# One 129-column product with v per key group, summed in two rounds per head, in an attention and channel-mix kernel on one core

## The chip, the core and the metric

The kernel runs on one core of a Trainium2 chip. Its time is device microseconds of one execution of the whole program, and each version is judged by the median of its runs. The profile is one more execution, recorded by the hardware profiler; times inside it are microseconds from the start of its span.

## The reference: what is computed

For 8 batches of 8 heads, queries are averaged in pairs (1152 to 576), attention runs against 1152 keys of 64 columns, and the result, 576 rows of 512 columns per batch, goes through a gated channel mix.

```python
q_pool = q.reshape(B, H, S // factor, factor, D).mean(axis=3)
scores = scale * np.matmul(q_pool, k.transpose(0, 1, 3, 2))
scores = scores - np.max(scores, axis=-1, keepdims=True)
attn = np.exp(scores)
attn = attn / (np.sum(attn, axis=-1, keepdims=True) + 1e-09)
attn_out = np.matmul(attn, v)
...
xk = mu_k * x + (1.0 - mu_k) * x_prev
xr = mu_r * x + (1.0 - mu_r) * x_prev
k = np.maximum(xk @ w_k, 0.0)
v = k * k @ w_v
r = 1.0 / (1.0 + np.exp(-(xr @ w_r)))
return (r * v).astype(np.float32)
```

## The kernel before

All inputs are float32; the matmuls take float16 operands, so each float32 factor is split into a high and a low half and a product is a sum of two or three matmuls.

**Order.** Every step is recorded with `op` (engine, an estimated duration, what it reads and writes, a due time `key`). At the end `Issue.run` plays the recorded steps against the estimated durations and hand-over times in `LAT`, in several rounds, keeps the order with the least planned total and issues every engine's instructions in that order. `LATE` and `SLACK` lengthen the estimates, `SEED` and `SPREAD` disturb the due times of the first round. Each engine then takes its instructions strictly in the planned order, so an instruction that waits holds back all behind it on its engine.

**Scores.** `block` handles 96 queries of one head against all 1152 keys (9 groups of 128); a head has 6 blocks, the program 384. TensorE forms the scores (L462, 9 matmuls of 96 columns) in one of three PSUM tiles `s`. VectorE takes the maximum over the key groups (L469), TensorE turns it (L472), VectorE reduces it to one value per query (L475), TensorE spreads its negative (L477), ScalarE writes it as a row of the low half of the queries (L480), TensorE adds the low products and the shift (L486), and ScalarE takes the exponential into `pf` (L492). `pf` holds 32-bit words whose upper 16 bits are read as the high float16 weight; GpSimd makes the low weight `pl` from the lower 16 bits (L494).

**Product with v.** `window` handles 128 queries; a head has 5 windows (`WIN`). Per key group, the high weights are loaded twice: once for a matmul of 65 columns (L513: the high half of v and a column of ones, whose sum is the denominator) and once for one of 64 columns (L515: the low half of v), both added into the same 65 columns of the PSUM bank `a`. The low weights multiply `vb`, a scaled float16 copy of v with its ones column, in 65 columns (L520). All five windows of a head lie side by side in the bank (5 x 65 = 325 columns). After the fifth, VectorE adds a guard to the denominators (L535), inverts them (L537) and writes the quotients to `xb` (L538). After every second head, TensorE turns the pair (L550) and ScalarE copies it to `xt` (L553). In the first batch (heads 0 to 7) the odd heads use the bank `f` instead (`ALT`).

**Preparation.** `prep` loads k and v of a head. ScalarE makes the high half `kn` (L415) and VectorE the rest (L418), in two pieces of 5 and 4 groups; for the first 8 heads GpSimd makes the rest (`KN_POOL`). `vt` holds v as [low 64 | high 64 | ones] (L428, L431), `vb` is made by GpSimd (L434).

**Weights.** `weights` loads the three weight matrices in 20 pieces of 512 64-bit numbers a row and rebuilds float32 from the two words: ScalarE L580 into `ex` and L587 into `em`, VectorE joins them (L590) and adds the sign (L598), ScalarE rounds to the high half (L600) and GpSimd makes the low half (L601). `ex` and `em` are in SBUF, two buffers each.

**Channel mix.** `ff` works on tiles of 256 rows as soon as a batch's attention is complete, so nothing of it can run during the first batch. Its matmuls of 256 and 512 columns (L665) go to the bank `f`, and after the last batch to all banks in turn. They are what TensorE has to do between the steps of the blocks.

## Time and profile before

| | |
|---|---|
| median of 3 runs | 1162.75 us (1162.2 to 1163.17) |
| the profiled execution, its own time | 1164.27 us |
| its span | 1162.5 us |
| granted TensorE clock, mean | 0.997 |
| TensorE matmuls | 19504, busy 1111.6 us (96%) |
| TensorE weight loads | 19504, busy 926.0 us (80%) |
| VectorE | 908.2 us busy (78%) |
| ScalarE | 888.7 us busy (76%) |
| GpSimd | 550.0 us busy (47%) |

In the profile PE is TensorE, PEld its weight loads, DVE VectorE, ACT ScalarE, POOL GpSimd and SP the engine that issues the transfers; L with a number is a line of the kernel. Matmuls are pipelined: the duration shown for one is from its start to its modelled end, and what a matmul takes of the engine is the distance between its start and the next one's. A row of the timeline is start, duration, engine, line, operation and operands, number merged. A row of the groups is line, engine, operation, operands with shapes, count, then busy time and mean duration in ns, then the engine's idle time just before and what ended it. A row of the windows is the stretch, its length, then each engine's busy time with its number of instructions, then the clock.

### The profile page before, as it was taken

The numbers are of one execution on the slowest core, as the hardware profiler recorded it, in microseconds if no ns is written. First come the engines' busy times: TensorE is split into PE (matmuls) and PEld (weight loads), VectorE is DVE, ScalarE is ACT, GpSimd is POOL, SyncE is SP. The second block draws the span as 40 slices with busy tenths as digits, with TensorE's granted clock in tenths as the row PEclk, the third lists the DMA queues.
The fourth block names the chain that finished last, engine by engine and source line by source line (L and its number), as shares of the span: only waits on it lengthen the run. The fifth ranks groups of instructions, "written<-read, shape, count | busy, mean of one in ns | idle before, by whom it ended". The sixth has DMA issues, their size and how long they took to land.

```text
span 1162.5 us, 45688 instructions
## 1 busy us (share of the span) xinstructions
PE 1111.6 (96%) x19504; PEld 926.0 (80%) x19504; DVE 908.2 (78%) x1791; ACT 888.7 (76%) x1838; POOL 550.0 (47%) x565
## 2 busy tenths in 40 slices
PE   4887799999999999999999999999999999999998
PEld 3776687978788887988788888979797978888565
DVE  6898878888888878888888878787888788774530
ACT  4988797887878788778877787878778778765743
POOL 4787554544445453544444453535354545443111
PEclk9999999999999999999999999999999999999999
DMA  9956663565545363564355536455554445310000
GB/s 233 219 143 175 155 135 78 134 130 126 129 99 114 94 143 98 134 123 106 90 109 120 132 81 145 85 117 115 113 123 86 95 112 93 70 30 10 20 19 28
DMA packets 222380, 126.69 MB, mean 109 GB/s; under 512 B 157664, under 2 KB 194528, under 8 KB 222176
## 3 DMA queue, kind: packets, MB, share of 16 engines
q1 hardware_dynamic: 222176, 123.77, 47.1%
q8 instruction: 152, 2.49, 0.9%
q14 instruction: 52, 0.43, 0.1%
HBM read 67.11 MB, written 9.44 MB: 66 GB/s over the span
## 4 chain that ended last, share of the span: by engine, by line
PE 85%; ACT 6%; DVE 3%; DMA 2%; issue 2%; POOL 1%; SPq 0%; DVEq 0%; ACTq 0%
PE f L665 33%; PE s L462 11%; PE s L486 11%; PE a L520 6%; PE a L515 6%; PE a L513 6%; PE s L665 4%; ACT pf L492 2%; PE s L472 2%; PE a L665 2%; DVE mx L469 1%; PE s L477 1%; PE a L550 1%; DMA st<-in_moe_w_k_dram 1%; ACT qT L480 1%
## 5 line engine op out<-in xcount | busy, mean ns | idle before, releaser
L494 POOL TENSOR_SCALAR pl<-pf 128x864 f16<-128x864 uint16 x384 | 385.0, 1003 | 405.4 <-ACT pf L492 378.3
L469 DVE TENSOR_REDUCE mx<-s 128x96 f16<-128x864 f32 x384 | 401.5, 1054 | 102.7 <-PE s L462 59.9
L492 ACT ACTIVATE pf<-s 128x864 int32<-128x864 f32 x384 | 337.4, 890 | 70.5 <-PE s L486 45.8
L462 PE MATMUL s<-qT,ks 128*128 128x96 f16 x3456 | 221.2, 207 | 28.6 <-DMA qT<-qn 15.1
L462 PEld LDWEIGHTS <-ks 128*128 128x128 f16 x3456 | 185.5, 99 | 54.6 <-issue 22.9
L515 PE MATMUL a<-vt,pf 128*128 128x64 f16 x2700 | 227.6, 194 | 0.0
L513 PE MATMUL a<-vt,pf 128*128 128x65 f16 x2700 | 227.2, 193 | 0.0
L486 PE MATMUL s<-qT,ks 128*128 128x96 f16 x3456 | 214.5, 207 | 7.2 <-ACT qT L480 6.7
L513 PEld LDWEIGHTS <-pf 128*128 128x128 f16 x2880 | 204.1, 99 | 6.0 <-ACT pf L492 0.4
L486 PEld LDWEIGHTS <-ks 128*128 128x128 f16 x3456 | 180.9, 98 | 28.5 <-issue 7.7
L515 PEld LDWEIGHTS <-pf 128*128 128x128 f16 x2880 | 194.8, 98 | 7.8 <-issue 0.3
L480 ACT ACTIVATE qT<-s 1x96 f16<-1x96 f32 x384 | 91.9, 243 | 99.8 <-PE s L477 87.6
L475 DVE TENSOR_REDUCE mb<-s 96x1 f16<-96x128 f32 x384 | 108.6, 285 | 57.9 <-PE s L472 53.3
L520 PE MATMUL a<-vb,pl 128*128 128x65 f16 x2700 | 143.4, 193 | 0.5 <-POOL pl L494 0.5
L665 PE MATMUL f<-xhk,wk_hi 128*128 128x256 f16 x496 | 135.1, 272 | 1.3 <-ACT xt L553 0.8
L665 PE MATMUL f<-xhk,wk_lo 128*128 128x256 f16 x496 | 135.1, 272 | 0.0
L665 PE MATMUL f<-xlk,wk_hi 128*128 128x256 f16 x496 | 135.1, 272 | 0.0
L520 PEld LDWEIGHTS <-pl 128*128 128x128 f16 x2880 | 121.8, 98 | 7.9 <-POOL pl L494 1.2
L696 POOL TENSOR_TENSOR gl<-g 128x512 f16<-128x512 f32 x72 | 78.5, 1090 | 100.7 <-ACT g L694 98.3
L665 PEld LDWEIGHTS <-wk_hi 128*128 128x128 f16 x1152 | 106.2, 98 | 11.6 <-issue 1.5
L472 PE MATMUL s<-identb,mx 128*96 128x128 f16 x384 | 87.1, 227 | 4.9 <-DVE mx L469 4.5
L665 PE MATMUL f<-wv_hi,g 128*128 128x512 f16 x240 | 90.9, 379 | 0.3 <-ACT ex L713 0.2
(101 smaller groups left out, 1990.2 us busy)
## 6 DMA issues: line engine op xcount, KB each, us to landing
kr<-in_k_dram SPq DMA_DIRECT2D x64, 288.0 KB, 3.3
vr<-in_v_dram SPq DMA_DIRECT2D x64, 288.0 KB, 3.1
qr<-in_q_dram SPq DMA_DIRECT2D x32, 320.0 KB, 3.7
ks<-ks SPq DMA_DIRECT2D x64, 144.0 KB, 2.8
out_dram<-em SPq DMA_DIRECT2D x36, 256.0 KB, 2.4
qr<-in_q_dram SPq DMA_DIRECT2D x32, 256.0 KB, 3.4
st<-in_moe_w_k_dram SPq DMA_DIRECT2D x8, 512.0 KB, 4.9
st<-in_moe_w_v_dram SPq DMA_DIRECT2D x8, 512.0 KB, 4.1
```

The costliest lines, as they stand in the source:

```text
L462: nc.tensor.matmul(cols(c, c + 1), ks1[hp][:, c, :], qhi, start=(c == c0), stop=False, skip_group_check=True)
L469: op("DVE", 0.967, lambda: nc.vector.tensor_reduce(mxz, grid(0, NC).rearrange("p c q -> p q c"), axis=AX.X, op=ALU.max), r=[("s", z)], w=[ ...
L472: op("PE", 0.057, lambda: nc.tensor.matmul(s[0:QN, 0:P], mxz, identb, start=False, stop=False, skip_group_check=True), r=[("mx", z)], w=[( ...
L475: op("DVE", 0.199, lambda: nc.vector.tensor_reduce(mbz[0:QN], s[0:QN, 0:P], axis=AX.X, op=ALU.max), r=[("s", z)], w=[("mb", z)], key=t + O ...
L480: op("ACT", 0.133, lambda: nc.scalar.activation(qlo[QN:QN + 1], s[QN:QN + 1, 0:QN], AF.Prelu, scale=1.0 - EPS, alpha=(1.0 + EPS) / (1.0 - ...
L486: nc.tensor.matmul(cols(c, c + 1), ks2[hp][:, c, :], qlo, start=False, stop=True, skip_group_check=True)
L492: op("ACT", NC * QN / 1200 + 0.051, lambda: nc.scalar.activation(pf[:, :, rows], grid(0, NC), AF.Exp, bias=SHIFT, scale=0.125 / (2.0 * SQ) ...
L494: op("POOL", NC * QN / 1000 + 0.12, lambda: nc.gpsimd.tensor_scalar(pl[:, :, rows], half(pf, U16, 0)[:, :, rows], LO, 1.0, op0=ALU.mult, o ...
L513: nc.tensor.matmul(bank[:, a0:a0 + VN], half(pf, F16, 1)[:, c, rows], vt[jv][:, c, D:D + VN], start=(w == 0 and c == 0), stop=False, skip_ ...
L515: nc.tensor.matmul(bank[:, a0:a0 + D], half(pf, F16, 1)[:, c, rows], vt[jv][:, c, 0:D], start=False, stop=False, skip_group_check=True)
L520: nc.tensor.matmul(bank[:, a0:a0 + VN], pl[:, c, rows], vb[jv][:, c, 0:VN], start=False, stop=(c == NC - 1), skip_group_check=True)
L665: nc.tensor.matmul(ps, terms[i][0], terms[i][1], start=(first and i == 0), stop=(i == last), skip_group_check=True)
```

## The change

It does five things at once.

1. From head 8 on (`SPLIT`), the two high matmuls per key group become one of 129 columns: v's low half, its high half and the ones are neighbours in `vt`. The low and the high half now stand in different columns, a window takes 129 columns, and a bank holds three windows. So a head is summed in two rounds, windows 0 to 2 and 3 to 4. After each, ScalarE copies the low columns to SBUF (`xlb`, L562), VectorE adds them to the high ones in PSUM (L564) and then divides (L566), with guard (L557) and inversion (L559) per round. The next round begins only when the bank has been read.
2. Heads 0 to 7 keep the two matmuls, but all of them use the bank `a` (`ALT` 0).
3. In those heads VectorE makes the rest of k (`KN_POOL` 0; 16 instructions move from GpSimd) and ScalarE makes `vb` (`VB_ACT`; 8 instructions move from GpSimd).
4. The weights are rebuilt through the bank `f`, which is idle in the first batch: the first ScalarE step writes there, VectorE joins there (L623) and adds the sign from there into `ex` (L626). There is one such bank, where `ex` and `em` have two buffers.
5. The planner's estimates, margins, seed and spread are others, so the whole order is new.

```diff
-LATE, SLACK = 0.08, 0.1
-KN_POOL, VT_POOL, XL_POOL = 8, 0, 0
-DEC_K, DEC_RV = "D", "D"
-ALT = 1
+LATE, SLACK = 0.04, 0.05
+KN_POOL, VT_POOL, XL_POOL = 0, 0, 0
+DEC_K, DEC_RV = 'S', 'S'
+ALT = 0
+VB_ACT = 8
+SPLIT = 8
...
-SEED, SPREAD = 2, 1.0
+SEED, SPREAD = 0, 3.0
...
+        if n < VB_ACT:
+            op("ACT", NC * D / 1200 + 0.093, lambda: nc.scalar.activation(
+                vb[j][:, :, 0:D], vr[i], AF.Copy, scale=SV * VLO), r=[("vr", i)], w=[("vb", j)], key=key + 4)
...
+        two = int(n >= SPLIT)
+        k0, k1 = [x[:2] for x in TURN if x[0] <= w < x[1]][0] if two else (0, NW)
+        VW = VN + two * D
+        a0, rows = (w - k0) * VW, slice(r0, r0 + P)
...
+                if two:
+                    nc.tensor.matmul(bank[:, a0:a0 + VN + D], half(pf, F16, 1)[:, c, rows], vt[jv][:, c, 0:VN + D],
+                                     start=(w == k0 and c == 0), stop=False, skip_group_check=True)
+                    continue
...
-        if w < NW - 1:
+        if w < k1 - 1:
             return
...
+        if two:
+            xl_ = xl_b[0][:, 0:k1 - k0]
+            op("ACT", 0.051 + (k1 - k0) * D / 1200, lambda: nc.scalar.copy(xl_, u[:, :, 0:D]),
+               r=[ka], w=[("xlb",)], key=t + O_EVAC)
+            op("DVE", 0.07 + (k1 - k0) * D / 960, lambda: nc.vector.tensor_tensor(
+                u[:, :, D:2 * D], u[:, :, D:2 * D], xl_, op=ALU.add), r=[ka, ("xlb",)], w=[ka], key=t + O_EVAC)
...
+                    ep, kf = f_b.bitcast(I32), ("f",)
...
+                    op("ACT", 0.52, lambda wh=wh: nc.scalar.activation(f_b, wh.bitcast(F32), AF.Abs, scale=2.0 ** -111),
+                       r=[ks], w=[kf], key=key)
...
+                        v_(0.6, lambda mi=mi, ep=ep: nc.vector.scalar_tensor_tensor(
+                            ep, ep, 3, mi, op0=ALU.logical_shift_left, op1=ALU.bitwise_or), [kf, km], [kf], False)
+                        kd, ed = (ke, e) if dec == "S" else (kf, f_b)
+                        v_(0.6, lambda ep=ep, wh=wh, ed=ed: nc.vector.scalar_tensor_tensor(
+                            ed.bitcast(I32), wh, -0x80000000, ep, op0=ALU.bitwise_and, op1=ALU.bitwise_or), [ks, kf], [kd], False)
```

Three places of the planned order show what moves. On TensorE, two key groups of one window of the product with v, in a later head, stood so before (`pf` are the weights that are loaded, `vt` what is multiplied):

```order
L513 LDWEIGHTS pf
L513 MATMUL a<-vt_86,pf 128x65
L515 LDWEIGHTS pf
L515 MATMUL a<-vt_86,pf 128x64
L513 LDWEIGHTS pf
L513 MATMUL a<-vt_86,pf 128x65
L515 LDWEIGHTS pf
L515 MATMUL a<-vt_86,pf 128x64
```

On TensorE now, the end of one window's high products and the first of its low ones:

```order
L531 LDWEIGHTS pf
L531 MATMUL a<-vt_87,pf 128x129
L531 LDWEIGHTS pf
L531 MATMUL a<-vt_87,pf 128x129
L541 LDWEIGHTS pl
L541 MATMUL a<-vb_90,pl 128x65
```

Four weight loads and four matmuls have become two of each; the low products are as they were.

On VectorE, the evacuation of head 30 before (`mx` and `mb` are the maxima of a block, `xb` the quotients):

```order
L475 TENSOR_REDUCE mb_96<-s_132 96x1
L535 TENSOR_SCALAR den_99<-a 128x5
L537 RECIPROCAL den_99<-den_99 128x5
L538 TENSOR_TENSOR xb_101<-a,den_99 128x5x64
L469 TENSOR_REDUCE mx_94<-s_133 128x96
```

On VectorE now, the first round of the same head (the second follows ten rows later with 2 windows in place of 3):

```order
L477 TENSOR_REDUCE mx_93<-s_133 128x96
L557 TENSOR_SCALAR den_99<-a 128x3
L701 TENSOR_TENSOR xlk_109<-xm_106,xhk_111 128x256
L559 RECIPROCAL den_99<-den_99 128x3
L564 TENSOR_TENSOR a<-a,xlb_102 128x3x64
L483 TENSOR_REDUCE mb_96<-s_133 96x1
L566 TENSOR_TENSOR xb_101<-a,den_99 128x3x64
L477 TENSOR_REDUCE mx_95<-s_135 128x96
```

Three steps per head have become eight, and other work stands between them.

On VectorE in the first batch, around the 18th block, before (`ex`, `em` and `st` belong to the weights):

```order
L469 TENSOR_REDUCE mx_95<-s_134 128x96
L590 SCALAR_TENSOR_TENSOR ex_120<-ex_120,em_122 128x512
L475 TENSOR_REDUCE mb_98<-s_134 96x1
L469 TENSOR_REDUCE mx_93<-s_132 128x96
L598 SCALAR_TENSOR_TENSOR ex_120<-st_124,ex_120 128x512
L475 TENSOR_REDUCE mb_96<-s_132 96x1
L469 TENSOR_REDUCE mx_94<-s_133 128x96
```

On VectorE now, around the same block:

```order
L477 TENSOR_REDUCE mx_95<-s_135 128x96
L483 TENSOR_REDUCE mb_97<-s_134 96x1
L422 TENSOR_TENSOR kn_76<-kr_70,kn_76 128x4x64
L435 SCALAR_TENSOR_TENSOR vt_86<-vr_72,vt_86 128x5x64
L483 TENSOR_REDUCE mb_98<-s_135 96x1
L435 SCALAR_TENSOR_TENSOR vt_86<-vr_72,vt_86 128x4x64
L623 SCALAR_TENSOR_TENSOR f<-f,em_123 128x512
L422 TENSOR_TENSOR kn_77<-kr_71,kn_77 128x5x64
L626 SCALAR_TENSOR_TENSOR ex_121<-st_125,f 128x512
L477 TENSOR_REDUCE mx_93<-s_133 128x96
```

The rest of k (L422) has come from GpSimd, and the weights pass through `f`.

More of the change, by code (lines that the diff above doesn't have):

```diff
@@ L465, in block @@
         for c0, c1 in BK:
-            op("PE", (c1 - c0) * 0.0424, lambda c0=c0, c1=c1: scores(c0, c1),
+            op("PE", (c1 - c0) * 0.0430, lambda c0=c0, c1=c1: scores(c0, c1),
                r=[("ks1", hp)] + kh, w=[("s", z)], key=t)
-        op("DVE", 0.967, lambda: nc.vector.tensor_reduce(mxz, grid(0, NC).rearrange("p c q -> p q c"),
+        op("DVE", 0.975, lambda: nc.vector.tensor_reduce(mxz, grid(0, NC).rearrange("p c q -> p q c"),
                                                          axis=AX.X, op=ALU.max),
            r=[("s", z)], w=[("mx", z)], key=t)
-        op("PE", 0.057, lambda: nc.tensor.matmul(s[0:QN, 0:P], mxz, identb, start=False, stop=False,
+        op("PE", 0.059, lambda: nc.tensor.matmul(s[0:QN, 0:P], mxz, identb, start=False, stop=False,
                                                  skip_group_check=True),
@@ L519, in lo @@
             for c in range(c0, c1):
-                nc.tensor.matmul(bank[:, a0:a0 + VN], pl[:, c, rows], vb[jv][:, c, 0:VN],
+                nc.tensor.matmul(bank[:, a0 + two * D:a0 + two * D + VN], pl[:, c, rows], vb[jv][:, c, 0:VN],
                                  start=False, stop=(c == NC - 1), skip_group_check=True)
         for c0 in (0, 3, 6):
-            op("PE", 3 * 0.0582, lambda c0=c0: hi(c0, c0 + 3),
-               r=vk + [("pf", j) for j in js] + ([ka] if c0 or w else []), w=[ka], key=t)
+            op("PE", 3 * (0.0565 if two else 0.0606), lambda c0=c0: hi(c0, c0 + 3),
+               r=vk + [("pf", j) for j in js] + ([ka] if c0 or w > k0 else []), w=[ka], key=t)
@@ L543, in window @@
-        for k0, k1, q0 in TURN:
-            base = WIN[k0][0]
-            qe = WIN[k1 - 1][0] + P
-            def turned(k0=k0, k1=k1, base=base):
-                for k_ in range(k0, k1):
+        dz, xz, d0 = den[z][:, k0:k1], xb[0][:, k0:k1], two * D
+        xk = [("xb", hh, x[0]) for x in TURN if k0 <= x[0] < k1]
+        op("DVE", 0.075, lambda: nc.vector.tensor_scalar(dz, u[:, :, d0 + D], GUARD, None, op0=ALU.add),
+           r=[ka], w=[("den", z, k0)], key=t + O_EVAC)
+        op("DVE", 0.08, lambda: nc.vector.reciprocal(dz, dz), r=[("den", z, k0)], w=[("den", z, k0)], key=t + O_EVAC)
@@ new lines, in window @@
+        if two:
[4 more added lines that the diff above has]
+                u[:, :, D:2 * D], u[:, :, D:2 * D], xl_, op=ALU.add), r=[ka, ("xlb",)], w=[ka], key=t + O_EVAC)
+        op("DVE", 0.07 + (k1 - k0) * D / 960, lambda: nc.vector.tensor_tensor(
+            xz[:, :, hh], u[:, :, d0:d0 + D], dz.unsqueeze(2).broadcast_to([P, k1 - k0, D]), op=ALU.mult),
+           r=[("den", z, k0), ka], w=xk, key=t + O_EVAC)
@@ L549, in turned @@
+        if hh == 0 or w < NW - 1:
+            return
+        for t0, t1, q0 in TURN:
+            base = WIN[t0][0]
+            qe = WIN[t1 - 1][0] + P
+            def turned(t0=t0, t1=t1, base=base):
+                for k_ in range(t0, t1):
                     r_ = WIN[k_][0] - base
-                    nc.tensor.transpose(bank[:, r_:r_ + P], xz[:, k_].rearrange("p h d -> p (h d)"), ident)
-            op("PE", 0.11 * (k1 - k0), turned, r=[("xb", 0), ("xb", 1)], w=[ka], key=t + O_TURN)
+                    nc.tensor.transpose(bank[:, r_:r_ + P], xb[0][:, k_].rearrange("p h d -> p (h d)"), ident)
+            op("PE", 0.113 * (t1 - t0), turned, r=[("xb", 0, t0), ("xb", 1, t0)], w=[ka], key=t + O_TURN)
@@ L581, in weights @@
+                op("ACT", 0.565, lambda e=e, wh=wh: nc.scalar.activation(e, wh.bitcast(F32), AF.Abs, scale=2.0 ** -111),
                    r=[ks], w=[ke], key=key)
@@ L688, in ff @@
                               (wlo["k"][:, c, fs], hk[:, c, 0:n], r)]
[L689 removed]
+                products(pv[:, f - f0], pk, terms, n / 2400.0 + 0.0025, first=(f == f0))
             z = turn("r32")
```

69 lines of the change are left out of this document (44 added, 25 removed).

## Prediction

> **What bounds the kernel now.** I read the windows first, cut where the channel mix begins and where the attention ends. The columns after the length are TensorE, its weight loads, VectorE, ScalarE, GpSimd, then the granted clock.
>
> ```profile
> 0.00:145.00 145.00, 103.10 (x2142) 92.98 (x2143) 121.69 (x227) 113.60 (x224) 94.50 (x101) 0.98 0.77 185
> 145.00:1075.00 930.00, 924.92 (x16845) 782.15 (x16843) 757.01 (x1506) 730.37 (x1521) 442.72 (x453) 1.00 0.48 105
> 1075.00:1162.50 87.50, 83.60 (x522) 50.88 (x520) 29.47 (x58) 44.69 (x95) 12.83 (x12) 1.00 0.06 24
> ```
>
> There are three stages. From 145 to 1075 us TensorE is busy 924.92 of 930 us; VectorE has 81% there and ScalarE 79%. The end is channel mix alone, again TensorE. In the first 145 us TensorE has 71% and VectorE leads with 84%. So a nanosecond off TensorE counts in full only after 145 us, and before that only the others count.
>
> Next the waits of TensorE inside the first 145 us (waited for: us, times, longest):
>
> ```profile
> PE s L462 <- DMA qT<-qn: 15.1, 1, 15.1
> PE s L462 <- ACT pf L492: 11.1, 22, 1.4
> PE s L486 <- ACT qT L480: 6.5, 12, 2.6
> PE s L472 <- DVE mx L469: 3.9, 8, 0.8
> ```
>
> After 15.1 us of loading, TensorE waits for the loop of a block itself: a free tile `s`, the written shift, the maximum. With three tiles, a block there advances as fast as VectorE and ScalarE take it round, and the channel mix is not there yet to fill in.
>
> Then the timeline of TensorE in the saturated stage, for what a matmul costs start to start:
>
> ```profile
> 602.00 0.27 PE L665 MATMUL f<-xhk,wk_lo 128*128 128x256 f16 x1
> ...
> 602.66 0.22 PE L472 MATMUL s<-identb,mx 128*96 128x128 f16 x1
> ...
> 604.24 0.19 PE L513 MATMUL a<-vt,pf 128*128 128x65 f16 x1
> 604.27 0.19 PE L515 MATMUL a<-vt,pf 128*128 128x64 f16 x1
> ...
> 604.60 0.44 PE L520 MATMUL a<-vb,pl 128*128 128x65 f16 x9
> 604.87 0.33 PE L462 MATMUL s<-qT,ks 128*128 128x96 f16 x4
> 605.04 0.55 PE L486 MATMUL s<-qT,ks 128*128 128x96 f16 x9
> 605.42 0.19 PE L513 MATMUL a<-vt,pf 128*128 128x65 f16 x1
> 605.45 0.20 PE L515 MATMUL a<-vt,pf 128*128 128x64 f16 x1
> ...
> 605.98 0.23 PE L472 MATMUL s<-identb,mx 128*96 128x128 f16 x1
> ```
>
> Six matmuls of 256 columns take 602.00 to 602.66, 110 ns each; nine of 96 columns 605.04 to 605.42, 42.2 ns; nine of 65 columns 604.60 to 604.87, 30.0 ns. The six pairs from 604.24 to 604.60 take 60.0 ns each, the nine pairs from 605.42 to 605.98 take 62.2 ns. Each of these matmuls has its own weight load, which by itself lasts 99 ns and overlaps the matmuls and loads before it:
>
> ```profile
> L513 PEld LDWEIGHTS <-pf 128*128 128x128 f16 x2880 | 204.1, 99 | 6.0 <-ACT pf L492 0.4
> ```
>
> **Part 1, the pairs.** 56 heads x 5 windows x 9 groups = 2520 pairs become single matmuls of 129 columns. No row has this width behind its own kind; the line through 96 and 256 columns rises (110 - 42.2) / 160 = 0.424 ns a column and gives 42.2 + 33 x 0.424 = 56.2 ns at 129. Against 60.0 the saving is 3.8 ns a pair, 9.6 us in all; against 62.2 it is 6.0 ns, 15.1 us. I take 12 us: the 65-column row at 30.0 speaks for the lower end, nine pairs against six for the upper. All of it lies after 145 us, on the path: **-12.0 us** (-9.6 to -15.1).
>
> The Trainium skill (TensorE: Matmul & The Clock Gate, section Back-to-back issue gap) gives about 81 ns per matmul at 128 columns in a stream of weight load and matmul; by that this part would be an estimated +50 us, not -12. The 42.2 ns row at 96 columns, each with its load, does not agree with it.
>
> **Part 2, what two rounds add in the saturated stage.** These rows carry it:
>
> ```profile
> L538 DVE TENSOR_TENSOR xb<-a,den 128x320 f32<-128x320 f32 x60 | 29.2, 487 | 1.3
> L729 DVE SCALAR_TENSOR_TENSOR em<-f,ex 128x512 f32<-128x512 f32 x30 | 20.7, 688 | 4.0 <-PE f L665 3.2 <-PE s L477 0.4
> L537 DVE RECIPROCAL den<-den 128x5 f32<-128x5 f32 x64 | 11.9, 186 | 1.4
> L535 DVE TENSOR_SCALAR den<-a 128x5 f32<-128x5 f32 x60 | 9.5, 158 | 11.4 <-PE a L520 10.5 <-PE s L477 0.4
> L553 ACT COPY xt<-a 128x384 f32<-128x384 f32 x28 | 13.4, 480 | 8.2 <-PE a L550 7.8
> L553 ACT COPY xt<-a 128x192 f32<-128x192 f32 x28 | 9.0, 322 | 1.9 <-PE a L550 1.5
> L513 PE MATMUL a<-vt,pf 128*128 128x65 f16 x2700 | 227.2, 193 | 0.0
> ```
>
> An elementwise step that reads PSUM costs 487 ns at 320 columns and 688 at 512: 1.05 ns a column, so 353 ns at 192 and 286 at 128. Per head VectorE gets two additions (639 ns), division in two pieces (639 in place of 487) and a second guard and inversion (344): 1.14 us, times 56 is 64 us. ScalarE gets a copy of 192 columns (322 ns) and one of 128 (by its two rows 269): 0.59 us, times 56 is 33 us. The stage then has VectorE at 821 of 918 us (89%) and ScalarE at 83%: both under TensorE, so the work itself costs nothing while TensorE has other matmuls queued.
>
> The wait is the question. The first product of the second round is queued on TensorE in order, and if the bank isn't read by then, all scores and channel mix behind it wait. The path of a round is copy 322, addition 353, division 353 ns and three hand-overs, about 1.2 us when both engines are free; up to 1.9 us more if a maximum and an exponential (about 1 us each) stand ahead. The cover is what the new order puts between the last low product of window 2 and the first product of window 3: counted in matmuls at the pitches above, 1.9 us in the worst two heads, 2.6 to 3.2 in twenty, median 3.5, up to 7.4. Before, the same bank between heads cost nothing (idle 0.0 ahead of L513). So no stall in most heads, some tenths in a few: 0 to 6 us, I take **+1.5 us**, near the row of zero.
>
> **Part 3, the first stage.** What moves in there, by these rows:
>
> ```profile
> L590 DVE SCALAR_TENSOR_TENSOR ex<-ex,em 128x512 int32<-128x512 int32 x20 | 16.0, 802 | 1.1 <-ACT ex L580 1.1
> L598 DVE SCALAR_TENSOR_TENSOR ex<-st,ex 128x512 int32<-128x512 int32 x20 | 14.4, 720 | 0.0
> L418 DVE TENSOR_TENSOR kn<-kr,kn 128x320 f16<-128x320 f32 x56 | 31.1, 555 | 0.9 <-ACT kn L415 0.8
> L418 DVE TENSOR_TENSOR kn<-kr,kn 128x256 f16<-128x256 f32 x56 | 25.3, 452 | 0.0
> L418 POOL TENSOR_TENSOR kn<-kr,kn 128x320 f16<-128x320 f32 x8 | 8.6, 1080 | 3.6 <-ACT kn L415 3.4
> L418 POOL TENSOR_TENSOR kn<-kr,kn 128x256 f16<-128x256 f32 x8 | 5.4, 676 | 1.9 <-ACT kn L415 1.5
> L434 POOL TENSOR_SCALAR vb<-vr 128x576 f16<-128x576 f32 x64 | 43.8, 684 | 73.9 <-PE a L520 45.7 <-PE s L477 13.0 <-DMA vr<-in_v_dram 8.4
> L385 ACT ACTIVATE qn<-qs 128x640 f16<-128x640 f32 x32 | 23.4, 733 | 3.3 <-DMA qT<-qn 2.1 <-DVE qs L382 1.0
> L636 DVE SCALAR_TENSOR_TENSOR xm<-xt,mu_k,tmp 128x256 f32<-128x256 f32 x48 | 27.9, 590 | 1.0 <-ACT tmp L633 0.5
> ```
>
> GpSimd loses 8 x (1080 + 676 + 684) ns = 19.5 us; it is at 65% there and gates little. VectorE gains 16 pieces of k, 8 x (555 + 452) = +8.1 us. The weights read one of their two operands from PSUM now; the nearest row for that is L729 at 688, so a piece costs 1.38 in place of 1.52 us. Up to the 54th maximum the new order has 19 pieces where the old has 16: 19 x 1.38 - 16 x 1.52 = +1.8 us; and five fewer steps of the mix (at the 590 of L636 or less), -2.7. VectorE's sum: +7.2 on 121.7 us. ScalarE gains 8 `vb` (about 0.68 each, a little under L385's 640 columns): +5.4.
>
> The Trainium skill (SBUF — State Buffer, section Who interferes with whom) says that a VectorE instruction with two SBUF inputs is held up by a GpSimd instruction that reads SBUF. The 802 of L590 against the 688 of L729 agrees: the rebuilt weights escape it, the 16 pieces of k enter it.
>
> If VectorE kept its share of 84%, 7.2 us of work would be 8.6 us of time; if the gaps take it, 0. The long runs of channel mix also begin later: before, they begin at the 55th block,
>
> ```profile
> 149.16 0.54 PE L462 MATMUL s<-qT,ks 128*128 128x96 f16 x9 [0.64 <-ACT pf L492]
> ```
>
> and in the new order with the 60th. A block of the first stage takes (149.16 - 15.1) / 54 = 2.48 us, and TensorE idles 29% of that: five more such blocks cost up to 3.6 us. Against this stands what a better order of the stage can save; the worst stretch of before is
>
> ```profile
> 90.00:100.00 10.00, 7.86 (x182) 7.24 (x183) 8.75 (x16) 9.29 (x18) 7.62 (x7) 1.00 0.74 189
> 100.00:110.00 10.00, 6.18 (x116) 5.47 (x114) 9.51 (x20) 7.46 (x18) 6.31 (x7) 0.91 0.74 193
> ```
>
> where TensorE falls to 6.18 of 10 us with VectorE at 9.51; without it some 2 us would be back, and with the relieved GpSimd perhaps as much again. Bounds: -4 to +12. I take **+5 us**, under half of 8.6 + 3.6, since VectorE had 16% of gaps. One bank `a` for the first eight heads and one bank `f` for the weights are counted in this range: evacuating took 0.8 us (158 + 186 + 487 ns) a head.
>
> **The sum.** -12.0 + 1.5 + 5.0 = -5.5 us. The profiled execution took 1164.27 us (span 1162.5), so it would take 1158.8; it stands 1.5 us above the median of the runs, so the forecast is 1157.2, said as **1157**.
>
> **The rivals.** (a) The first stage is not longer, or shorter: VectorE's gaps take the extra work and the relieved GpSimd hands `pl` over sooner. For it: nothing waits long for VectorE there (3.9 us). Then 1164.3 - 12 + 1.5 - (0 to 4) - 1.5 = 1148 to 1152 us. (b) Slower: VectorE bounds the first eight heads. With its use unchanged, 7.2 us of work and the later fill give the whole 12.2, and from VectorE above 90% on, a few more for each maximum that stands behind a piece of k; then -12 + 1.5 + 14 = +3.5, 1166 us. It decides where the first stage loses more than 12 - 1.5 = 10.5 us, which is 3.6 of later fill and a block of 2.6 us in place of 2.48. For it: VectorE at 84% and 9.51 of 10 in the worst stretch; against it: GpSimd's and TensorE's waits are shorter. (c) The evacuation in mid-head stalls TensorE: if the path takes 3.3 us as a rule, 24 heads wait some 0.5 us each, 11.6 us in all in place of 1.5: -12 + 11.6 + 5 = +4.6, 1167 us. Against it: the order leaves 3.5 us at the median, and before, the steps of an evacuation add up to 0.8. (d) The weight load is no longer hidden behind the one longer matmul and sets its pitch, 99 ns: 2520 x (99 - 61) = +96 us and the rest as forecast, about 1265 us. Against it: today two loads and two matmuls go by in 61 ns.
>
> **How the numbers follow.** The forecast's case (1152 to 1161) has 0.55, (a) 0.20, (b) 0.16, (c) 0.07, (d) 0.02. About 0.2% (2.3 us) is what a measurement of this kernel can tell from no change. Faster: 0.49 of the forecast's 0.55 and all of (a), 0.69. Same: 0.06 of the forecast's, 0.04 of (b), 0.02 of (c), 0.12. Slower: the rest of (b), (c) and (d), 0.19. The range 1146 to 1166 reaches down to (a) with a larger saving per pair and up to (b); (d) and half of (c) and of (b) lie outside.
>
> **What would show it.** Right: the new L531 stands 56 ns apart and the stage after the first batch takes about 10 us less; TensorE's share there stays over 99%; idle ahead of L531 is at most 1.5 us; VectorE near 89% there. The 60th block begins by 166 us, at most 5 us after the place that the old pace gives it, 15.1 + 59 x 2.48 = 161 us. Wrong: a pitch over 60 ns; waits of L531 for VectorE of 5 us or more; a first stage over 12 us longer or shorter than said.

## The result, and the profile after

| | before | after |
|---|---|---|
| median of the runs shown with the result | 1162.47 us (1162.0 to 1163.17, 4 runs) | 1174.91 us (1173.58 to 1177.36, 4 runs) |
| ratio | | 1.0108 (95%: 1.0095 to 1.0120) |
| profiled execution | 1164.27, span 1162.5 | 1174.88, span 1173.1 |
| granted clock, mean | 0.997 | 0.989 |
| TensorE matmuls | 19504 | 16984 |

The change makes the kernel 12.4 us slower; 1157 us was forecast, with 1166 as the end of the range. The engine totals of the page after read:

```profile
PE 1116.5 (95%) x16984; PEld 920.7 (78%) x16984; DVE 943.8 (80%) x2087; ACT 913.5 (78%) x1958; POOL 522.8 (45%) x541
```

VectorE is busy 35.6 us longer, ScalarE 24.8, GpSimd 27.2 less. The same three windows as before (stretch, length, busy time of TensorE, its loads, VectorE, ScalarE and GpSimd, clock, DMA share, GB/s):

```profile
0.00:145.00 145.00, 103.29 (x2117) 93.85 (x2118) 121.59 (x241) 118.54 (x233) 70.31 (x78) 0.93 0.77 192
145.00:1075.00 930.00, 919.29 (x14236) 768.64 (x14236) 789.71 (x1776) 745.22 (x1622) 437.34 (x450) 1.00 0.47 104
1075.00:1173.10 98.10, 93.97 (x634) 58.20 (x631) 32.47 (x70) 49.78 (x106) 15.18 (x15) 0.99 0.06 22
```

In the saturated stage TensorE is idle 10.7 of 930 us, where it was 5.1. VectorE stands at 85% there, ScalarE at 80%: neither is full. The wider matmul itself does what was asked of it; the timeline of TensorE in a late head shows nine of them in a row:

```profile
709.52 0.44 PE L541 MATMUL a<-vb,pl 128*128 128x65 f16 x9
709.80 0.67 PE L531 MATMUL a<-vt,pf 128*128 128x129 f16 x9
710.31 0.44 PE L541 MATMUL a<-vb,pl 128*128 128x65 f16 x9
710.58 0.23 PE L480 MATMUL s<-identb,mx 128*96 128x128 f16 x1
```

From 709.80 to 710.31 is 56.7 ns each; over the whole trace the mean is 56.6. The Trainium skill (TensorE: Matmul & The Clock Gate, section Back-to-back issue gap) also gives, for the gap of a matmul by itself, a rule of columns divided by 2.4 GHz plus 2.5 ns, an estimated 56.3 ns here. The trace agrees with it at 56.6, although each of these matmuls has its own weight load.

What TensorE waits for between 170 and 1062 us (engine, line, waited for: us, times, longest; the loads are the first to feel a wait). Before:

```profile
PEld L462 <- issue: 2.4, 7, 0.5
PEld L472 <- DVE mx L469: 2.2, 6, 0.6
PEld L486 <- issue: 1.8, 6, 0.4
PEld L477 <- DVE mb L475: 1.0, 2, 0.7
...
PE s L472 <- DVE mx L469: 0.7, 2, 0.4
PE s L477 <- DVE mb L475: 0.6, 1, 0.6
```

After:

```profile
PEld L470 <- issue: 7.6, 23, 0.7
PEld L494 <- issue: 5.5, 21, 0.7
PEld L480 <- DVE mx L477: 5.3, 17, 0.7
PEld L485 <- DVE mb L483: 4.1, 14, 0.7
PEld L531 <- issue: 2.2, 6, 0.8
...
PEld L531 <- DVE xb L566: 0.7, 3, 0.4
```

The loads of the same four steps of a block (both score products, the turning of the maxima and the spreading of the negative) wait 22.5 us where they waited 7.4. Of the 22.5, 13.1 stand as issue, for which the profile names no cause, and 9.4 are waits for the two maxima. The loads of the new matmul L531, where the forecast looked for a stall, wait 2.9. The waits of the four steps are short, 0.3 us at the mean and 0.7 at most, and spread over the stage.

**An account of the whole span.** From the starts of all matmuls I worked out how much each step from one matmul to the next is longer than the measured pitches, the distances from start to start, allow (0.417 ns a column + 2.5 ns, which gives the 42.5, 109.2 and 215.8 ns measured at 96, 256 and 512 columns; twice that for a float32 transpose). "Need" is the sum of these pitches, "idle" the rest (time lost to a lower clock is in it), cut at the 61st block, the first of the second batch (170.2 us before, 176.7 after); 108 channel-mix matmuls had been issued by then in both.

| us | start | idle to the 61st block | idle after it | of that in gaps of 25 ns and more | need | end | span |
|---|---|---|---|---|---|---|---|
| before | 15.1 | 52.9 | 18.2 | 9.4 (50 gaps) | 1071.9 | 4.3 | 1162.5 |
| after | 15.4 | 56.8 | 30.8 | 25.7 (144 gaps) | 1065.6 | 4.5 | 1173.1 |
| difference | +0.3 | +3.9 | +12.6 | +16.3 | -6.3 | +0.2 | +10.6 |

The matmuls give back 10.0 us (6.3 of need and 3.7 in gaps under 25 ns, 8.8 to 5.1). The gaps above 25 ns take 16.3, the first stage 3.9.

**A wait that nobody had asked for.** Of VectorE's waits between 170 and 1075 us, these are the four longest in the changed kernel:

```profile
DVE mx L477 <- PE s L470: 39.7, 58, 3.4
DVE mb L483 <- PE s L480: 20.6, 49, 1.0
DVE den L557 <- ACT xlb L562: 18.0, 26, 1.2
DVE den L557 <- PE a L541: 12.2, 17, 3.3
```

The guard L557 reads the denominators and the copy L562 the low columns, both from the bank `a`. No data passes from one to the other, yet the guard waits 18.0 us for the copy. One such place on the timeline:

```profile
585.44 0.89 ACT L500 ACTIVATE pf<-s 128x864 int32<-128x864 f32 x1
...
585.95 0.44 PE L541 MATMUL a<-vb,pl 128*128 128x65 f16 x9
...
586.35 0.24 ACT L488 ACTIVATE qT<-s 1x96 f16<-1x96 f32 x1
...
586.62 0.27 ACT L562 COPY xlb<-a 128x128 f32<-128x128 f32 x1
...
586.92 0.16 DVE L557 TENSOR_SCALAR den<-a 128x2 f32<-128x2 f32 x1 [1.06 <-ACT xlb L562]
587.00 1.06 DVE L477 TENSOR_REDUCE mx<-s 128x96 f16<-128x864 f32 x1
```

The last low products end at 586.39. ScalarE finishes an exponential and writes a shift first, copies at 586.62, and only then, at 586.92, does the guard start; the next block's maximum stands behind the guard on VectorE and starts at 587.00. The Trainium skill (PSUM — Partial Sum Buffer, section PSUM bank collisions raise a hardware error) says that ScalarE and VectorE may not be on one bank, in the same group of 32 partitions, at once, two reads included, and that a compiler therefore puts a dependency between them. The 18.0 us of waits in this trace agree; the prediction did not have them.

### The profile page after: what moved, and what is told of

Same layout as the page of the kernel before. It is cut to its first block, busy times and chain, and to the rows that moved or that the text cites. A ratio compares the mean times of both kernels' runs of the same rounds, so it can differ in the third digit from the quotient of the medians.

```text
span 1173.1 us, 40929 instructions
## 1 busy us (share of the span) xinstructions
PE 1116.5 (95%) x16984; PEld 920.7 (78%) x16984; DVE 943.8 (80%) x2087; ACT 913.5 (78%) x1958; POOL 522.8 (45%) x541
## 4 chain that ended last, share of the span: by engine, by line
PE 74%; ACT 9%; DVE 4%; issue 2%; POOL 0%; ACTq 0%; DVEq 0%; POOLq 0%
PE f L722 30%; PE a L531 11%; PE s L494 9%; PE s L470 9%; PE a L541 6%; PE s L722 4%; ACT pf L500 4%; DVE mx L477 2%; PE a L722 2%; PE s L480 1%; PE s L485 1%; ACT qT L488 1%; PE a L578 1%; ACT tmp L690 1%; ACT qn L389 0%
## 5 line engine op out<-in xcount | busy, mean ns | idle before, releaser
L508 POOL TENSOR_SCALAR pl<-pf 128x864 f16<-128x864 uint16 x384 | 378.3, 985 | 459.0 <-ACT pf L500 425.1
L470 PE MATMUL s<-qT,ks 128*128 128x96 f16 x3456 | 219.4, 208 | 29.0 <-DMA qT<-qn 15.4
L470 PEld LDWEIGHTS <-ks 128*128 128x128 f16 x3456 | 187.9, 99 | 61.0 <-issue 21.8
L494 PEld LDWEIGHTS <-ks 128*128 128x128 f16 x3456 | 184.0, 99 | 32.1 <-issue 13.3
L531 PE MATMUL a<-vt,pf 128*128 128x129 f16 x2520 | 206.1, 220 | 1.7 <-ACT xt L581 1.1
L531 PEld LDWEIGHTS <-pf 128*128 128x128 f16 x2520 | 158.0, 98 | 13.5 <-issue 2.2
L541 PE MATMUL a<-vb,pl 128*128 128x65 f16 x2880 | 149.4, 193 | 0.1
L722 PE MATMUL f<-wv_hi,gl 128*128 128x512 f16 x240 | 90.9, 379 | 0.0
L722 PE MATMUL f<-wv_lo,g 128*128 128x512 f16 x240 | 90.9, 379 | 0.0
```

What stands on the lines that cost most here:

```text
L470: nc.tensor.matmul(cols(c, c + 1), ks1[hp][:, c, :], qhi, start=(c == c0), stop=False, skip_group_check=True)
L494: nc.tensor.matmul(cols(c, c + 1), ks2[hp][:, c, :], qlo, start=False, stop=True, skip_group_check=True)
L508: op(pe, d, lambda: en.tensor_scalar(pl[:, :, rows], half(pf, U16, 0)[:, :, rows], LO, 1.0, op0=ALU.mult, op1=ALU.mult), r=[("pf", j)], w= ...
L531: nc.tensor.matmul(bank[:, a0:a0 + VN + D], half(pf, F16, 1)[:, c, rows], vt[jv][:, c, 0:VN + D], start=(w == k0 and c == 0), stop=False, ...
L541: nc.tensor.matmul(bank[:, a0 + two * D:a0 + two * D + VN], pl[:, c, rows], vb[jv][:, c, 0:VN], start=False, stop=(c == NC - 1), skip_grou ...
L722: nc.tensor.matmul(ps, terms[i][0], terms[i][1], start=(first and i == 0), stop=(i == last), skip_group_check=True)
```

## The experiments

The first question was what the copy and the addition cost within the changed kernel's own order. Its order is kept in the first two kernels. `e1_copy_sbuf` lets ScalarE copy zeros of SBUF, so that only VectorE touches the bank (the low columns are missing from the sum):

```diff
+    xl_z = const.tile([P, 3, D], F32, name="xlz")
...
-            op("ACT", 0.051 + (k1 - k0) * D / 1200, lambda: nc.scalar.copy(xl_, u[:, :, 0:D]),
+            op("ACT", 0.051 + (k1 - k0) * D / 1200, lambda: nc.scalar.copy(xl_, xl_z[:, 0:k1 - k0]),
```

> The order of every engine as in the changed kernel (but for one memset at the start); the ScalarE copy of each round reads a buffer of zeros in SBUF in place of the bank, so the low columns are left out of the sum. Same steps, same load, but VectorE's guard no longer shares its bank with that copy. Theory W (the guard waits for the copy, which the plan does not know; 18.0 us in 26 waits, and the maxima behind it come late): the waits go, TensorE's gaps after the first batch fall from about 26 to about 12 us, 1160 to 1165 us. Theory L (VectorE and ScalarE are too full, 87 and 81%): within 2 us of 1175. Theory M (the planner's margins are too thin): within 2 us of 1175.

Measured: 1169.74 us, ratio 1.0065 (1.0049 to 1.0082). The guard's waits, in the same view as above:

```profile
DVE mx L479 <- PE s L472: 42.7, 71, 3.4
...
DVE den L559 <- PE a L543: 19.6, 25, 4.0
DVE a L566 <- ACT xlb L564: 6.8, 19, 0.8
```

The wait of the guard for the copy is gone, the addition's own wait for the copied data is left, and the time falls by 5.2 us against the changed kernel. That is neither the 1160 to 1165 us of theory W nor the 1175 of the other two. The edit also frees the copy from waiting for the products and the guard, so what it prices is the reading of the bank as a whole. By the account above, only 3.1 us of the gain lie behind the 61st block (idle 27.7 in place of 30.8); the rest is an earlier start (0.9) and the first stage (1.0), which the copy hardly touches. So the bank is worth some 3 to 5 us.

`e2_no_low` issues neither the copy nor the addition, in the same order (the low columns are left out):

```diff
-            op("ACT", 0.051 + (k1 - k0) * D / 1200, lambda: nc.scalar.copy(xl_, u[:, :, 0:D]),
+            op("ACT", 0.051 + (k1 - k0) * D / 1200, lambda: None,
...
-            op("DVE", 0.07 + (k1 - k0) * D / 960, lambda: nc.vector.tensor_tensor(
-                u[:, :, D:2 * D], u[:, :, D:2 * D], xl_, op=ALU.add), r=[ka, ("xlb",)], w=[ka], key=t + O_EVAC)
+            op("DVE", 0.07 + (k1 - k0) * D / 960, lambda: None, r=[ka, ("xlb",)], w=[ka], key=t + O_EVAC)
```

> The planned order of the changed kernel with the ScalarE copy and the VectorE addition of each round not issued, so the low columns are left out of the sum. Takes the wait and the load of both away. Theories W and L: 1158 to 1164 us; the part that this gains over the run in which only the bank is no longer shared is the load's. Theory M: 1172 to 1175 us, since the thin margins stay.

Measured: 1164.07 us, ratio 1.0020 (1.0008 to 1.0032): 10.8 us less than the changed kernel. Its ten runs spread from 1162.65 to 1168.19 us, and the profile is of the longest. TensorE's waits between 170 and 1062 us:

```profile
PEld L470 <- issue: 5.9, 18, 0.7
PEld L494 <- issue: 3.4, 14, 0.7
PEld L480 <- DVE mx L477: 2.6, 10, 0.5
PEld L485 <- DVE mb L483: 1.8, 7, 0.4
```

All four block steps wait less, 13.7 us in place of 22.5: the copy and the addition reach TensorE through the blocks. By the account, idle behind the 61st block falls by 8.5 us, from 30.8 to 22.3. That leaves this kernel still 1.6 us above the one before, although it has the cheaper matmuls.

`e5_pairs` keeps the changed kernel's order, rounds, copies and additions, and splits each wide matmul again:

```diff
-                    nc.tensor.matmul(bank[:, a0:a0 + VN + D], half(pf, F16, 1)[:, c, rows], vt[jv][:, c, 0:VN + D],
+                    nc.tensor.matmul(bank[:, a0 + D:a0 + D + VN], half(pf, F16, 1)[:, c, rows], vt[jv][:, c, D:D + VN],
                                      start=(w == k0 and c == 0), stop=False, skip_group_check=True)
+                    nc.tensor.matmul(bank[:, a0:a0 + D], half(pf, F16, 1)[:, c, rows], vt[jv][:, c, 0:D],
+                                     start=False, stop=False, skip_group_check=True)
```

> The changed kernel with its order and its two rounds, but with two matmuls (65 and 64 columns, into neighbouring columns) in place of each of the 2520 of 129. Prices the fusion alone. The pitches of the traces (60.8 ns a pair, 56.6 ns now) give 4.2 x 2520 = 10.6 us if TensorE is the bound throughout: 1184 to 1187 us. If half of that is swallowed by waits for VectorE and ScalarE: 1179 to 1182. If the stage is bound by those two: 1174 to 1177.

Measured: 1181.32 us, ratio 1.0162 (1.0145 to 1.0179), 6.4 us above the changed kernel. Behind 145 us, where all the changed pairs stand, a pair took 60.4 ns before (the 60.8 above is over the whole trace, with the first heads in it), so the pitch says 3.8 ns x 2520 = 9.6 us. Of these, 6.4 come out in an order where TensorE has to wait anyway.

**The order.** The next two ask whether the planner's estimates are at fault. `e3_margins` gives the changed kernel the old margins, `e4_told` tells the planner that the guard follows the copy:

```diff
-LATE, SLACK = 0.04, 0.05
+LATE, SLACK = 0.08, 0.1
```

> The changed kernel with the planner's margins of before (LATE 0.08, SLACK 0.1), so another order. Theory M: 1160 to 1165 us. Theories W and L: 1171 to 1179 us, no better than chance among orders.

```diff
-        op("DVE", 0.075, lambda: nc.vector.tensor_scalar(dz, u[:, :, d0 + D], GUARD, None, op0=ALU.add),
-           r=[ka], w=[("den", z, k0)], key=t + O_EVAC)
...
         if two:
             xl_ = xl_b[0][:, 0:k1 - k0]
             op("ACT", 0.051 + (k1 - k0) * D / 1200, lambda: nc.scalar.copy(xl_, u[:, :, 0:D]),
                r=[ka], w=[("xlb",)], key=t + O_EVAC)
+        op("DVE", 0.075, lambda: nc.vector.tensor_scalar(dz, u[:, :, d0 + D], GUARD, None, op0=ALU.add),
+           r=[ka] + [("xlb",)] * two, w=[("den", z, k0)], key=t + O_EVAC)
...
```

> The changed kernel, with the planner told that the guard comes after the copy: the step is recorded behind it and reads its result in the plan. All else as in the change, a new order. Theory W: the guard's waits for ScalarE fall under 5 us and the time to 1160 to 1166 us. Theories L and M: 1172 to 1178 us.

Measured: 1177.48 us, ratio 1.0130 (1.0115 to 1.0145), and 1176.04 us, ratio 1.0120 (1.0105 to 1.0135). Neither helps. In `e4_told` the guard still waits 22.9 us for the copy, 23 times between 145 and 1080 us: an order that allows for the wait does not make it short.

`e7_split_off` is the changed kernel with items 2 to 5 of the change and no fusion; `e6_split_alone` has the fusion and all other settings as before (the planner's new estimates of durations stay):

```diff
-SPLIT = 8
+SPLIT = 64
```

> The changed kernel without the fusion and its two rounds: two matmuls into the same columns, one round per head, all else as changed. If the two rounds cost all that was lost: 1160 to 1164 us. If the other parts (first batch, weights, a new order) cost some 12 us: 1172 to 1177 us.

```diff
-LATE, SLACK = 0.04, 0.05
-KN_POOL, VT_POOL, XL_POOL = 0, 0, 0
-DEC_K, DEC_RV = 'S', 'S'
-ALT = 0
+LATE, SLACK = 0.08, 0.1
+KN_POOL, VT_POOL, XL_POOL = 8, 0, 0
+DEC_K, DEC_RV = 'D', 'D'
+ALT = 1
...
-VB_ACT = 8
+VB_ACT = 0
...
-SEED, SPREAD = 0, 3.0
+SEED, SPREAD = 2, 1.0
```

> The kernel before with the fusion and its two rounds alone (from head 8 on): bank f for the odd heads of the first batch, pieces of k and vb on GpSimd, weights rebuilt in SBUF, margins, seed and spread as before; the estimates of the new code. If the two rounds cost what the two runs without them showed (5.2 + 5.6 us) and the fusion saves 10.6: 1160 to 1165 us, and the rest of the loss belongs to the other parts. If the two rounds cost all of it: 1172 to 1177 us.

Measured: 1176.63 us, ratio 1.0123 (1.0107 to 1.0138), and 1179.74 us, ratio 1.0151 (1.0136 to 1.0167). Each half of the change alone is as slow as the whole, and the fusion alone slower than either of its two expectations. Two halves that each lose what the whole loses are no sum of costs; what the two kernels have in common is that the planner made a new order for each. (An order that one set of planner numbers gives is called a draw below.) So three kernels take the kernel before, step for step, and change nothing but planner numbers: all four of them (`e8_planner`), the seed (`e9_seed`), the margins (`e10_margins`).

```diff
-LATE, SLACK = 0.08, 0.1
+LATE, SLACK = 0.04, 0.05
...
-SEED, SPREAD = 2, 1.0
+SEED, SPREAD = 0, 3.0
```

> The kernel before, with the changed margins, seed and spread of the planner alone (LATE 0.04, SLACK 0.05, SEED 0, SPREAD 3.0): the same instructions in another order. If the order of before was worth little: 1161 to 1165 us. If a new order by itself costs several us: 1167 to 1174 us, and TensorE's gaps after the first batch rise from about 10 to over 15 us.

```diff
-SEED, SPREAD = 2, 1.0
+SEED, SPREAD = 0, 1.0
```

> The kernel before with SEED 0 in place of 2 and nothing else: the same instructions, margins and spread, another order. Theory O (the order of before is a good draw, and another one costs some 10 to 20 us whatever stands in it): 1170 to 1182 us. Theory M (the thinner margins did it) or S (the spread of 3.0 did it): 1160 to 1166 us.

```diff
-LATE, SLACK = 0.08, 0.1
+LATE, SLACK = 0.04, 0.05
```

> The kernel before with the margins of the change (LATE 0.04, SLACK 0.05), seed and spread as before. Theory M: 1175 to 1185 us. Theory O: also a new order, so anywhere from 1165 to 1182 us, without a link to the margins; alone it tells little, beside the run with another seed it does. Theory S: 1160 to 1165 us.

Measured: 1183.22 us, ratio 1.0179 (1.0164 to 1.0194); 1171.31 us, 1.0075 (1.0061 to 1.0088); 1175.74 us, 1.0108 (1.0093 to 1.0124). Planner numbers alone, with the same instructions, cost 9 to 21 us; all four together cost more than the 1174 us that had been thought the most. Two more seeds of the kernel before, `e15_before_seed1` and `e16_before_seed3`, and three other draws of the changed kernel complete the picture: `e12_after_seed2` (its margins, seed 2, spread 1), `e17_after_seed1` (margins 0.08 and 0.1, seed 1, spread 1) and `e18_after_seed2` (all four numbers as before the change).

```diff
-SEED, SPREAD = 2, 1.0
+SEED, SPREAD = 1, 1.0
```

> The kernel before with SEED 1 and nothing else. Theory O (the order of before is a good draw): 1168 to 1184 us, as with seed 0 or other margins. If seed 0 was a bad draw: 1161 to 1165 us.

```diff
-SEED, SPREAD = 2, 1.0
+SEED, SPREAD = 3, 1.0
```

> The kernel before with SEED 3 and nothing else. Theory O: 1168 to 1184 us. If the order of before is an ordinary draw: 1160 to 1166 us.

```diff
-SEED, SPREAD = 0, 3.0
+SEED, SPREAD = 2, 1.0
```

> The changed kernel with the seed and spread of before (2 and 1.0). Theory O: another draw, anywhere from 1165 to 1185 us. Theory S: 1160 to 1166 us. If the two rounds and the first batch bound the kernel, not the order: 1173 to 1177 us.

```diff
-LATE, SLACK = 0.04, 0.05
+LATE, SLACK = 0.08, 0.1
...
-SEED, SPREAD = 0, 3.0
+SEED, SPREAD = 1, 1.0
```

> The changed kernel with margins and spread of before and SEED 1. Theory O with steps that nearly cancel: 1168 to 1180 us, within the spread of the draws of the kernel before. If the changed steps are worth the 11 us that the pitches give and the order alone is the loss: its draws should lie some 10 us under those of before, 1158 to 1172.

```diff
-LATE, SLACK = 0.04, 0.05
+LATE, SLACK = 0.08, 0.1
...
-SEED, SPREAD = 0, 3.0
+SEED, SPREAD = 2, 1.0
```

> The changed kernel with all planner numbers of before (margins 0.08 and 0.1, SEED 2, SPREAD 1.0); its steps differ, so it is another order none the less. Theory O with steps that nearly cancel: 1168 to 1180 us. If the numbers of the planner themselves were the loss: 1150 to 1163 us.

Measured, with the four cases in which both kernels ran with the same planner numbers side by side:

| margins, seed, spread | steps of before | steps of after | difference |
|---|---|---|---|
| 0.08/0.1, 2, 1 (shipped before) | 1162.5 | 1167.76, ratio 1.0035 (1.0022 to 1.0048) | +5.3 |
| 0.08/0.1, 1, 1 | 1180.26, ratio 1.0150 (1.0135 to 1.0165) | 1174.59, ratio 1.0097 (1.0080 to 1.0114) | -5.7 |
| 0.04/0.05, 2, 1 | 1175.74 | 1170.14, ratio 1.0063 (1.0050 to 1.0077) | -5.6 |
| 0.04/0.05, 0, 3 (shipped after) | 1183.22 | 1174.91 | -8.3 |
| 0.08/0.1, 3, 1 | 1182.04, ratio 1.0163 (1.0147 to 1.0179) | | |
| 0.08/0.1, 0, 1 | 1171.31 | | |
| 0.08/0.1, 0, 3 | | 1177.48 | |

Six draws of the old steps lie between 1162.5 and 1183.2, five of the new ones between 1167.8 and 1177.5. The shipped order of before is the best of all eleven, 5.3 us ahead of the next and 8.8 ahead of the next one with its own steps. Between the shipped pair lie -8.3 us for the changed steps and +20.7 for the changed numbers, if taken in this sequence; in the other sequence +5.3 and +7.1. (The kernel before ran at 1162.9 us beside the first of the changed ones; by that its difference is +4.9.) The mean of the four differences is -3.6, with a scatter of some 6 us: its sign isn't settled by four. Over all draws, the old steps take 1175.8 us at the mean and the new ones 1173.0. So the shipped order of before lies 13.3 us under the mean of its own draws, and the shipped order after 1.9 above its own.

Where a bad draw loses is seen in the account: `e16_before_seed3` is idle 64.7 us up to the 61st block, `e15_before_seed1` 65.6, where the shipped order has 52.9; behind it 23.6 and 23.5 against 18.2. In the first 145 us of `e16_before_seed3` TensorE and VectorE have got less done than in the shipped order (103.10 and 121.69):

```profile
0.00:145.00 145.00, 95.62 (x2058) 86.19 (x2058) 109.06 (x206) 106.09 (x206) 87.72 (x97) 0.97 0.68 167
```

The same account of all eleven profiles sets the steps against the draw. Behind the 61st block the six draws of the old steps are idle 18.2, 21.1, 23.5, 23.6, 26.8 and 28.1 us, 23.6 at the mean; the five of the new steps 28.6, 29.4, 30.1, 30.8 and 31.2, 30.0 at the mean. Every draw of the new steps is idle longer there than any of the old, and the 6.4 us more at the mean take up the 6.3 us that the fusion saves in need. Not all of it need come from the rounds: `e7_split_off`, which has items 2 to 5 without the fusion, is idle 30.0 us there in its one draw. Up to the 61st block the two sets overlap (52.9 to 65.6 and 54.2 to 60.1 us).

**With the order held.** Three kernels keep the order of before and change only what is issued in it. `e11_two_fused` fuses the first two of the five windows from head 8 on (two windows of 129 and three of 65 columns are 453, and fit the bank, so there is one round); VectorE makes the copy and the addition inside the old division step:

```diff
+                if w < nf:
+                    nc.tensor.matmul(bank[:, a0:a0 + VN + D], half(pf, F16, 1)[:, c, rows], vt[jv][:, c, 0:VN + D],
+                                     start=(w == 0 and c == 0), stop=False, skip_group_check=True)
+                    continue
...
+                nc.vector.tensor_copy(xl_b[0], uf[:, :, 0:D])
+                nc.vector.tensor_tensor(uf[:, :, D:2 * D], uf[:, :, D:2 * D], xl_b[0], op=ALU.add)
+                nc.vector.tensor_tensor(xz[:, 0:nf, hh], uf[:, :, D:2 * D],
+                                        dz[:, 0:nf].unsqueeze(2).broadcast_to([P, nf, D]), op=ALU.mult)
```

> The order of before kept word for word (the planner sees the same steps), with two of the five windows of a head from head 8 on as 129 columns and three as pairs, 453 columns in one round; copy, addition and a second guard and division are issued on VectorE inside the steps that evacuate, which makes that some 0.7 us a head longer. Theory O: the fusion pays in a good order; 1008 pairs at 2.5 to 4.2 ns, 2.5 to 4.2 us less, 1158 to 1160 us. If VectorE's extra work or the fusion itself were the harm: 1163 us or more.

`e14_fused_no_low` is the same without the first two of these VectorE steps (the low columns of those two windows are left out):

```diff
-                nc.vector.tensor_copy(xl_b[0], uf[:, :, 0:D])
-                nc.vector.tensor_tensor(uf[:, :, D:2 * D], uf[:, :, D:2 * D], xl_b[0], op=ALU.add)
```

> The order of before, two of five windows fused from head 8 on, without the copy and the addition, so the low columns of these windows are left out of the sum; a second guard and a second division stay (about 0.2 us a head). Theory D: the 1008 fused pairs pay 2.5 to 4.2 us, the remaining steps cost some 2 to 4: 1160 to 1164 us, 4 to 7 less than with copy and addition. Theory F: 1167 us and over, as with them.

`e13_dve_only` keeps the pairs and adds, from head 8 on, two VectorE steps of that size, whose result equals what was there:

```diff
+                nc.vector.tensor_copy(xl_b[0], u[:, 0:2, 0:D])
+                nc.vector.tensor_tensor(u[:, 0:2, 0:D], u[:, 0:2, 0:D], xl_b[0], op=ALU.max)
```

> The order of before kept word for word, all pairs kept, nothing fused; from head 8 on the step that divides also copies 128 columns of the bank to SBUF and takes the maximum of the two equal values, which changes no result: some 0.45 us more on VectorE per head (25 us in all), while VectorE is about 82% busy there. Theory D (a static order has no slack for VectorE, each added step delays the maximum behind it and TensorE stands): 1167 to 1172 us, with gaps ahead of the turning and spreading of the maximum. Theory F (VectorE's idle share takes the steps, and it is the fusion that hurts): 1162 to 1164 us.

Measured: `e11_two_fused` 1167.85 us, ratio 1.0052 (1.0039 to 1.0065); `e14_fused_no_low` 1159.15 us, ratio 0.9969 (0.9957 to 0.9981); `e13_dve_only` 1168.23 us, ratio 1.0047 (1.0032 to 1.0062). Without the addition, 1008 fused pairs bring 3.5 us, a second guard and a second division included; their pitch says 3.8 ns x 1008 = 3.8. With it, 8.7 us come on top. A copy and a second step of that size without any fusion cost 5.6. So theory O's 1158 to 1160 us did not come; what theory D expected of the last two did, `e14_fused_no_low` a little under its range. What VectorE has more of is seen in one window, 170 to 1060 us. Before:

```profile
170.00:1060.00 890.00, 886.46 (x16258) 751.24 (x16256) 732.20 (x1460) 701.11 (x1463) 424.78 (x437) 1.00 0.48 106
```

`e11_two_fused`:

```profile
170.00:1060.00 890.00, 881.54 (x15176) 741.99 (x15173) 764.88 (x1664) 696.66 (x1454) 426.67 (x434) 1.00 0.48 105
```

VectorE has 764.88 in place of 732.20 us, 86% in place of 82% of the 890; in `e13_dve_only` it has 757.06, 24.9 us more. TensorE's waits between 170 and 1062 us in `e13_dve_only`, then in `e14_fused_no_low`:

```profile
PEld L473 <- DVE mx L470: 5.1, 13, 0.9
PEld L478 <- DVE mb L476: 3.8, 9, 0.9
...
PE s L478 <- DVE mb L476: 1.7, 3, 0.8
PE s L473 <- DVE mx L470: 1.4, 3, 0.7
```

```profile
PEld L463 <- issue: 2.3, 8, 0.4
PEld L473 <- DVE mx L470: 2.2, 6, 0.6
PEld L487 <- issue: 2.1, 7, 0.4
PEld L478 <- DVE mb L476: 1.1, 2, 0.7
...
PE s L473 <- DVE mx L470: 0.7, 2, 0.4
PE s L478 <- DVE mb L476: 0.6, 1, 0.6
```

The waits for the two maxima are 12.0 us against 4.6 (before: 4.5). Between `e13_dve_only` and before only VectorE's evacuation differs, so the late maxima come from the steps that now stand ahead of them there, on an engine that is busy 85% of the time. (These orders were not planned for the added steps; one that is may lose less, or more.)

## Why the prediction was wrong

**Part 1, the pairs: right, the saving a little too large.** -12.0 us forecast, -9.6 by the pitches (56.2 ns estimated, 56.6 measured; 60.4 for a pair behind 145 us, near the lower of the two rows) and -10.0 in the account. It is worth 6.4 us in the changed kernel's order (`e5_pairs`).

**Part 2, two rounds in the saturated stage: the step that failed.** The prediction put it so: VectorE at 89% and ScalarE at 83% are "both under TensorE, so the work itself costs nothing while TensorE has other matmuls queued", and took +1.5 us, at most 6. The idle time behind the 61st block grew by 12.6 us, the gaps in it by 16.3. At the mean of the draws, too, the stage keeps nothing of Part 1: 6.4 us more of idle time stand beside 6.3 less of need. The durations were right:

```profile
L564 DVE TENSOR_TENSOR a<-a,xlb 128x192 f32<-128x192 f32 x56 | 20.1, 358 | 2.2 <-ACT xlb L562 1.4
L566 DVE TENSOR_TENSOR xb<-a,den 128x192 f32<-128x192 f32 x56 | 19.4, 347 | 0.2
L562 ACT COPY xlb<-a 128x192 f32<-128x192 f32 x56 | 17.9, 319 | 6.9 <-PE a L541 2.9 <-DVE den L557 2.4 <-PE s L480 0.9
L557 DVE TENSOR_SCALAR den<-a 128x3 f32<-128x3 f32 x56 | 8.7, 155 | 19.1 <-ACT xlb L562 10.2 <-PE a L541 7.6 <-PE s L480 0.7
```

358, 347 and 319 ns stand against 353, 353 and 322 in the forecast. (The 64 us were added to a busy time, though: VectorE's durations add up to 62 us more over the trace, 1064.9 after 1002.8, but some overlap, and its busy time grew by 35.6.) The place was looked at rightly as well: the second round's first product waits almost never, as the median cover of 3.5 us said, and rival (c) did not happen. None of the signs that the prediction named for being wrong came up; they watched L531 and the first stage, and the loss came at the blocks. What failed is the conclusion from use to cost. TensorE takes its matmuls in the planned order, and behind the turning of a late maximum stands everything else, channel mix too. In a fixed order 25 us of added VectorE work cost 5.6 us (`e13_dve_only`), and in the changed kernel's order the copy and addition cost 10.8 (`e2_no_low`; 8.5 of them behind the 61st block), of which some 3 to 5 hang on both engines reading one bank (`e1_copy_sbuf`). The second guard, the second inversion and the second division were not tried by themselves.

**Part 3, the first stage: the size about right, perhaps by luck.** +5 us forecast; +3.9 of idle time measured up to the 61st block, and the 60th block began at 161.8 us, where 161 to 166 was said. A piece of the weights took 1.36 us (687 + 675 ns), where 1.38 was said. Rival (b), with its +14 in the first stage, did not happen. How much of the 3.9 is due to the moved work, how much to the draw and how much to the clock stays open: draws of the old steps alone range from 52.9 to 65.6 us in this stage, and the lower clock told of in the last section, which the forecast did not have, could by itself be more than 3.9 (8.8 us against 3.2). The prediction's reading of the 802 ns of L590 is not settled either: L720 of the kernel before has two SBUF operands too and took 683 ns at the same width.

**A term that was put at nothing: the order itself.** Item 5 of the change stood in the text, but its cost was taken as nothing beyond the places examined. The old kernel's order is a good draw; the same steps with five other sets of planner numbers take 1171 to 1183 us. All ten other orders are slower, by some 5 us at least. With the order held, the full fusion of two windows loses 5.2 us (`e11_two_fused`), so a bad draw is not the whole reason; with the old planner numbers the whole change loses some 5 (`e18_after_seed2`). Under the three other sets of numbers the changed steps gain 5.6 to 8.3. Against the means of the draws, the 12.4 us are mostly the good draw that was given up (13.3), and the steps come out 2.9 us better, less than the draws scatter. Shown is that added VectorE work costs time in a fixed order, and that at the mean of the draws the saturated stage gains nothing; how the 12.4 us of this pair of orders divide is not settled. No version with the whole sum beat the kernel before; the only faster one, `e14_fused_no_low`, lacks the addition that the fusion needs.

**The rest.** The stage behind the first batch, which was to take about 10 us less, takes 4.1 more (from the 61st block to the end of the span, 996.4 us after 992.3). TensorE's share behind 145 us is 98.8%, where over 99% was said; idle time ahead of L531 is 1.7 us in its group, where at most 1.5 was said; VectorE stands at 85% in place of 89%. Rival (d) did not happen: the matmuls with one weight load each stand 56.6 ns apart, not 99.

## What to carry to other kernels

An engine at 80% in a stage that another one bounds is no free room if the bounding engine takes its instructions in a fixed order: price added steps by what stands behind them, or try them alone in the old order, where 25 us of such work cost 5.6 here. When a search sets the order, time a few draws of the unchanged kernel first; a spread of 20 us covers a gain of 10. And when two engines share an evacuation, look whether they read one PSUM bank: the guard waited 18.0 us in all for a copy whose data it didn't need.
